# Column sums of a second softmax on VectorE's 32x32 transposes, and engine orders read from a table

## The chip, the cores and the metric

The kernel runs on one core of one Trainium2 chip. The metric is the device time of one execution in microseconds (us), median of several runs. The core's engines each work through a program of their own: TensorE (PE, with weight loads as PEld), VectorE (DVE), ScalarE (ACT), GpSimd (POOL) and SyncE (SP); they wait for each other by semaphores. POOL issues the loads from memory, SP issues the stores and the transposing copies.

## The reference

A two-stage attention is followed by a two-layer network with a quadratic knee as its activation. Shapes: 8 batches, 8 heads, 576 tokens of 64 channels, 32 landmark rows `p` per head; the network has widths 512, 2048, 512.

```python
def sm_attn(qq, kk, vv):
    s = scale * np.matmul(qq, kk.transpose(0, 1, 3, 2))
    s = s - np.max(s, axis=-1, keepdims=True)
    a = np.exp(s)
    a = a / (np.sum(a, axis=-1, keepdims=True) + 1e-09)
    return np.matmul(a, vv)
p_packed = sm_attn(p, k, v)
attn = sm_attn(q, p_packed, p_packed)
x = attn.transpose(0, 2, 1, 3).reshape(B * S, H * D)
h = x @ w_in
g = np.where(h >= 1, h, np.where(h <= -1, 0.0, (h + 1) ** 2 / 4))
out = g @ w_out
```

The second softmax is the one that the change touches: for each of 576 tokens and each of 8 heads it sums 32 numbers.

## The kernel before

**What is computed per batch.** The keys are brought into a transposed layout (`kT`), multiplied with the landmarks (tile `sp` or `s1`), and an exponential on ACT gives `ex` or `exn`. The packed values `pk` (32 rows per head) are copied to `ppT`, and their reciprocal sums are `rs`. From `ppT` two products are formed on PE: `mp`, the packed values already multiplied with `w_in`, which ACT or VectorE copies to `M`; and `s2` (shown as `s` in the profile), the second scores, 128 partitions by 576. The 128 partitions of `s2` are four heads times 32 landmarks, so the eight heads make two groups `g`. Partitions hold landmarks, the free axis holds the tokens. ACT takes `eT = exp(s2)` (line 723). The sum of a softmax runs here over 32 partitions of one head: PE multiplies `eT` with `onesblk`, a matrix of four 32x32 blocks of ones, which puts the sum on all 32 partitions (`sm`, line 728: two matmuls of 288 columns per group); ACT takes `ln` of it (line 732) and `rc = exp(-ln)` (line 737); VectorE forms `A = eT * rs * rc` (line 742).

**The hidden layer and the output.** For each of 16 slices `fi` of the hidden width PE forms `h` (line 814, four matmuls of 288 columns, reading `M` and `A`); ACT forms `x` from it (line 820); `t` is made from `x` by VectorE (line 828) or by ACT (line 830); VectorE writes `hT` (line 835). An output tile of 128 tokens is 16 matmuls `o` (line 889, 512 columns each, reading `hT` and `w_out_sb`), then a copy to `ob` (line 271, either engine) and a store on SP. There are 36 such tiles, 9 for each pair of batches; those of a pair run while the next batches are prepared. Buffers: three of two banks each in PSUM for `h`, `sm`, `s2`, `mp`, `pk` and others, two of one bank for `o`; four each of `x`, `t`, `eT` and `ob`.

**What sets the order.** Nothing is scheduled at run time. When the program is built, a planner (class `Plan`, lines 25 to 180) gives each step a rank, a length on each engine that may do it, its dependencies and its buffers, and picks the next step of each engine among those that are ready; ties within 0.05 us go by rank. The ranks come from the tables `AT`, `HID` and `OUT` (lines 228 to 244). The steps are emitted in the order of their planned starts, and each engine runs its own in that order. Before the first `o`, gaps of PE's plan are filled with matmuls on zeros (`warm`, line 939).

Of the kernel before, what the change touches and what calls it, by code (L numbers as in the profile page):

```python
# [11 lines left out]
class Task:  # L12
# [4 lines left out]
    def __init__(self, rank, ways, deps=(), takes=(), mode=None, behind=()):  # L17
        self.rank, self.ways, self.deps = rank, ways, list(deps)
        self.behind = [d for d in behind if d is not None]
        self.takes, self.frees, self.mode = list(takes), [], mode  # L20
        self.start = self.end = self.engine = None
        self.users = []


class Plan:
# [8 lines left out]
    CLAIM = 0.3  # L34
# [4 lines left out]
    def __init__(self, buffers):  # L39
# [8 lines left out]
    def add(self, rank, ways, deps=(), takes=(), mode=None, behind=()):  # L48
        t = Task(rank, ways, deps, takes, mode, behind)
        self.tasks.append(t)  # L50
        return t
# [38 lines left out]
    def run(self, slack):  # L90
        waiting = {id(t): len(t.deps) + len(t.behind) for t in self.tasks}
        started = defaultdict(list)
# [5 lines left out]
        ready = [t for t in self.tasks if not waiting[id(t)]]  # L98
        done = []

        def served(users):
            for u in users:
                waiting[id(u)] -= 1
                if waiting[id(u)] == 0:
                    ready.append(u)

        def finished(t):
# [5 lines left out]
            served(t.users)  # L113

        while len(done) < len(self.tasks):
            best = None
            found = defaultdict(list)
            left = {b: sorted(v) for b, v in self.slots.items()}
            for t in sorted(ready, key=lambda t: t.rank):
                at = max((d.end + self.LATENCY for d in t.deps), default=0.0)  # L120
                at = max([at] + [d.start + 0.001 for d in t.behind])
                need = defaultdict(int)
                for b in t.takes:
                    need[b] += 1
                short = any(len(left[b]) < n for b, n in need.items())
                wants = at < self.free["PE"] + self.CLAIM
                for b, n in need.items():
                    if not short:
                        at = max(at, left[b][n - 1] + self.LATENCY)
                    if wants:  # L130
                        del left[b][:n]
                if short:
                    continue
                for e in t.ways:
                    if e == "SP" and self.held is not None:
                        continue
                    start = max(self.free[e], at)
                    if e == "PE" and self.mode is not None and t.mode != self.mode:
                        start = max(start, self.free[e] + self.SWITCH)
                    found[e].append((start, t))  # L140
            for e, some in found.items():
                first = min(x[0] for x in some)
                at, t = min((x for x in some if x[0] <= first + slack.get(e, 0.0)), key=lambda x: (x[1].rank, x[0]))
# [7 lines left out]
            assert best is not None, "no step can take its buffers"  # L151
            at, t, e = best
            if e == "PE" and t.mode != self.mode:
                at = max(at, self.free[e] + self.SWITCH)
            ready.remove(t)
            keep, lasts = t.ways[e][:2]
            t.start, t.engine, t.end = at, e, at + lasts
# [6 lines left out]
            served(started[id(t)])  # L164
# [19 lines left out]
def kernel(  # L184
# [38 lines left out]
    SPLIT, AHALF, WPARTS, MPARTS, QLATE, ORDER3, ORDER = 2, 1, 1, 0, 1, 0, 2  # L223
# [3 lines left out]
    L1 = 15.967  # L227
    AT = [dict(kT=148.161, qT=275.48, sc=149.063, pk=-49.085, s2=-3.905, sm=-182.602, M=178.569, **{"M+": -129.863}),
          dict(kT=-39.644, qT=-48.123, sc=-66.351, pk=124.743, s2=170.079, sm=-187.478, M=-105.149, **{"M+": 146.812}),
          dict(kT=115.732, qT=51.477, sc=130.42, pk=237.931, s2=-181.084, sm=-29.758, M=169.369, **{"M+": -44.412}),  # L230
          dict(kT=29.446, qT=-25.092, sc=52.472, pk=243.839, s2=179.754, sm=-32.11, M=115.586, **{"M+": -71.343}),
          dict(kT=38.536, qT=86.402, sc=153.04, pk=258.796, s2=-13.152, sm=-43.327, M=-95.344, **{"M+": 110.184}),
          dict(kT=1.864, qT=113.754, sc=282.551, pk=400.409, s2=-26.009, sm=-92.874, M=125.845, **{"M+": 0.958}),
          dict(kT=126.633, qT=239.492, sc=-4.526, pk=382.024, s2=-90.437, sm=32.434, M=177.14, **{"M+": -62.453}),
          dict(kT=27.261, qT=148.76, sc=40.741, pk=216.362, s2=-45.985, sm=130.271, M=1.019, **{"M+": -201.613})]
    HID = [(27.4, 1.3921), (-10.054, 2.601), (22.49, 3.9747), (126.895, 4.8485), (231.121, 9.6612), (-18.141, 4.6461), (3.622, 15.8949), (451.41, 5.8147)]
    OUT = [[(235.954, -183.0), (268.544, -106.533), (35.947, 20.528), (122.624, -48.891)],
# [24 lines left out]
    plan = Plan(dict(BUFS, dma=8, exn=1))  # L262
# [52 lines left out]
    consts = plan.add(-1000, {"DVE": (2.4, 2.4, constants)})  # L315

    identity = plan.add(-998.5, {"POOL": (0.6, 1.25, lambda e: make_identity(nc, ident))})
# [3 lines left out]
    last_of = {"loads": identity}  # L321
# [8 lines left out]
    def dma(key, rank, emit, mb, takes=(), settle=0.9):  # L330
        t = plan.add(rank, {"DMA": (0.78, 2.1, emit, mb / 0.405, settle)}, takes=list(takes) + ["dma"])
        plan.release("dma", [t])
        chain("loads", t)
# [14 lines left out]
    def load(nm, b, rank):  # L348

        for i, hs in enumerate({("k", 0): [range(4, 8)], ("q", 0): Q0}.get((nm, b), [range(H)])):  # L350
# [3 lines left out]
            t = dma((nm, b, hs[0]), rank + 0.01 * i, emit, mb, [nm] if i == 0 else [], 0.9 if b < 2 else 1.1)  # L354
# [3 lines left out]
    def load_w_in(f, rank):  # L358

        parts = [(0, D), (D, P)] if WPARTS and f == 0 else [(0, P)]  # L360
        for i, (p0, p1) in enumerate(parts):
            dma(("w_in", f) + (i,) * (len(parts) - 1), rank + 0.01 * i,
# [4 lines left out]
    def load_w_out(f, rank):  # L367
# [610 lines left out]
```

## Time and profile before

| what | value |
|---|---|
| median of 3 runs | 244.42 us (243.48 to 244.64) |
| profiled execution, span from first to last instruction | 241.1 us |
| own time of the profiled execution | not on the page; the median of the runs lies 3.3 us above the span |
| instructions | 5370 |
| DVE busy, ACT busy in the 21.7 us behind 219.4 us | 3.69 us, 5.85 us |

A row of groups gives line, engine, operation, what is written and read, the count, then the busy time in us and the mean length of one in ns, then how long the engine sat idle just before them and what ended that. A row of the timeline or of the chain gives start and length in us. The length of one matmul contains its way through the array, so rows of several matmuls tell their rate: 33 matmuls `o` take 7.12 us, 0.2158 us each.

### The profile page before, as it was taken

The numbers are of one execution on the slowest core, as the hardware profiler recorded it, in microseconds if no ns is written. First come the engines' busy times: TensorE is split into PE (matmuls) and PEld (weight loads), VectorE is DVE, ScalarE is ACT, GpSimd is POOL, SyncE is SP. The second block draws the span as 40 slices with busy tenths as digits, with TensorE's granted clock in tenths as the row PEclk, the third lists the DMA queues.
The fourth block names the chain that finished last, engine by engine and source line by source line (L and its number), as shares of the span: only waits on it lengthen the run. The fifth ranks groups of instructions, "written<-read, shape, count | busy, mean of one in ns | idle before, by whom it ended". The sixth has DMA issues, their size and how long they took to land.

```text
span 241.1 us, 5370 instructions
## 1 busy us (share of the span) xinstructions
PE 233.3 (97%) x2117; PEld 133.9 (56%) x2154; DVE 177.6 (74%) x311; ACT 192.7 (80%) x342; POOL 31.4 (13%) x47
## 2 busy tenths in 40 slices
PE   8999999999999999999999999999999999999995
PEld 2646555466554665466645564465546644565454
DVE  4549997678967998789936898689999955899000
ACT  3779996988969985999776988999789988888111
POOL 8462006200220040030030003000000000000000
PEclk9999999999999999999999999999999999999999
DMA  7999999996999999999999999999930301202233
GB/s 158 196 206 207 206 205 205 197 241 132 125 198 149 234 164 251 152 221 221 194 165 246 233 141 147 161 141 226 191 94 4 85 5 44 71 21 65 65 87 90
DMA packets 64138, 37.03 MB, mean 154 GB/s; under 512 B 36720, under 2 KB 59632, under 8 KB 64112
## 3 DMA queue, kind: packets, MB, share of 16 engines
q0 software_dynamic: 24336, 18.25, 52.6%
q1 hardware_dynamic: 38960, 17.87, 36.7%
q10 hardware_dynamic: 816, 0.56, 0.8%
q8 instruction: 17, 0.28, 0.5%
q14 instruction: 9, 0.07, 0.1%
HBM read 37.22 MB, written 9.44 MB: 194 GB/s over the span
## 4 chain that ended last, share of the span: by engine, by line
PE 81%; DVE 6%; DMA 5%; ACT 4%; POOL 2%; issue 2%; POOLq 0%; ACTq 0%
PE o L889 48%; PE h L814 21%; DMA w_in_sb<-in_moe_w_in_dram 5%; DVE hT L835 4%; PE mp L686 3%; PE pk L619 2%; PE sm L728 1%; DVE t L828 1%; ACT x L820 1%; PE sp L528 1%; PE s L700 1%; ACT t L830 1%; POOL q L352 1%; ACT M L271 1%; PE o L942 1%
## 5 line engine op out<-in xcount | busy, mean ns | idle before, releaser
L889 PE MATMUL o<-w_out_sb,hT 128*128 128x512 bf16 (+2 forms) x574 | 140.9, 367 | 1.9 <-issue 0.6
L835 DVE SCALAR_TENSOR_TENSOR hT<-t 128x576 bf16<-128x576 f32 (+1 forms) x130 | 93.7, 746 | 4.3 <-ACT t L830 2.3
L820 ACT ACTIVATE x<-h 128x576 f32<-128x576 f32 (+1 forms) x130 | 78.6, 651 | 9.1 <-PE h L814 8.5
L889 PEld LDWEIGHTS <-hT 128*128 128x128 bf16 x608 | 55.8, 98 | 49.8 <-issue 6.1
L814 PE MATMUL h<-A,M 128*128 128x288 bf16 x512 | 78.5, 286 | 0.6 <-ACT M L271 0.3
L814 PEld LDWEIGHTS <-M 128*128 128x128 bf16 x512 | 49.9, 98 | 27.6 <-issue 1.1
L830 ACT ACTIVATE t<-x 128x576 f32<-128x576 f32 (+1 forms) x57 | 39.4, 693 | 0.6
L828 DVE TENSOR_SCALAR t<-x 128x576 f32<-128x576 f32 (+1 forms) x73 | 33.3, 456 | 7.1 <-ACT x L820 6.7
L271 ACT COPY ob<-o 128x512 f32<-128x512 f32 (+2 forms) x22 | 12.0, 552 | 17.0 <-PE o L889 16.9
L742 DVE SCALAR_TENSOR_TENSOR A<-eT,rs,rc 128x576 bf16<-128x576 bf16 (+1 forms) x18 | 12.8, 748 | 11.5 <-ACT rc L737 11.5
L271 ACT CAST M<-mp 128x1024 bf16<-128x1024 f32 (+1 forms) x20 | 19.1, 992 | 2.7 <-PE mp L686 2.7
L352 POOL DMA_DIRECT2D k<-in_k_dram x8 | 6.7, 843 | 87.8 <-DMA kT<-k 68.4
L271 DVE CAST M<-mp 128x1024 bf16<-128x1024 f32 (+1 forms) x13 | 15.3, 1180 | 3.1 <-PE mp L686 3.1
L271 DVE COPY ob<-o 128x512 f32<-128x512 f32 x16 | 10.8, 688 | 6.9 <-PE o L889 6.9
L723 ACT ACTIVATE eT<-s,rs 128x576 bf16<-128x576 f32 x16 | 11.1, 742 | 2.5 <-PE s L700 2.5
L942 PE MATMUL o<-zeros 128*128 128x512 bf16 (+1 forms) x35 | 10.5, 431 | 1.3 <-DVE zeros L307 1.2
L732 ACT ACTIVATE ln<-sm 128x576 f32<-128x576 f32 x16 | 10.3, 652 | 1.2 <-PE sm L728 0.7
L686 PE MATMUL mp<-w_in_sb,ppT 64*32 64x512 bf16 x256 | 10.9, 380 | 0.2
L271 ACT CAST ppT<-pk 64x128 bf16<-64x128 f32 x24 | 6.2, 260 | 5.7 <-PE pk L634 4.0
L737 ACT ACTIVATE rc<-ln 128x576 f32<-128x576 f32 (+1 forms) x18 | 10.4, 625 | 0.1
L352 POOL DMA_DIRECT2D v<-in_v_dram x8 | 6.2, 779 | 21.9 <-PE pk L624 15.2
L533 ACT ACTIVATE ex<-sp 96x768 bf16<-96x768 f32 (+1 forms) x12 | 8.1, 709 | 0.5 <-PE sp L528 0.4
(59 smaller groups left out, 116.7 us busy)
## 6 DMA issues: line engine op xcount, KB each, us to landing
v<-in_v_dram POOLq DMA_DIRECT2D x8, 576.0 KB, 11.6
out_dram<-ob SPq DMA_DIRECT2D x23, 192.0 KB, 4.5
k<-in_k_dram POOLq DMA_DIRECT2D x7, 576.0 KB, 8.7
q<-in_q_dram POOLq DMA_DIRECT2D x7, 576.0 KB, 12.8
out_dram<-ob SPq DMA_DIRECT2D x24, 128.0 KB, 2.9
w_out_sb<-in_moe_w_out_dram POOLq DMA_DIRECT2D x4, 512.0 KB, 19.7
w_in_sb<-in_moe_w_in_dram POOLq DMA_DIRECT2D x3, 512.0 KB, 15.2
out_dram<-ob SPq DMA_DIRECT2D x23, 64.0 KB, 4.5
```

The costliest lines, as they stand in the source:

```text
L271: i = (nc.vector.tensor_copy if e == "DVE" else nc.scalar.copy)(to, of)
L352: G_.dma_start(tokens(nm, b)[:, heads(hs)], rows_of(nm, b, hs))
L686: m = nc.tensor.matmul(have["mp", b, f][a * NP:(a + 1) * NP, g], have["ppT", b][r, g, a], w_in_sb[r, a, f * FW:(f + 1) * FW], start=True, ...
L723: nc.scalar.activation(have["eT", b, g], have["s2", b, g][:, :, :HALF], AF.Exp, scale=rs_of[b][:, g, 1:])
L742: V.scalar_tensor_tensor(have["A", b][:, g, xs], have["eT", b, g][:, xs], rs_of[b][:, g, :1], have["rc", b, g][:, xs], ALU.mult, ALU.mult)
L814: nc.tensor.matmul(have["h", b, fi][:, hf, :HALF], have["M", b][:, g, fi * P:(fi + 1) * P], have["A", b][:, g, hf], start=(g == 0), stop=( ...
L820: nc.scalar.activation(have["x", b, fi][:, hs[0]:hs[-1] + 1], have["h", b, fi][:, hs[0]:hs[-1] + 1, :HALF], AF.Prelu, bias=-1.0, alpha=0.5)
L828: V.tensor_scalar(t, x, 1.0, 0.0, ALU.add, ALU.max)
L830: nc.scalar.activation(t, x, AF.Relu, bias=1.0)
L835: V.scalar_tensor_tensor(dst, t, 1.0, t, ALU.min, ALU.mult)
L889: nc.tensor.matmul(have["o", key][:, :w], hT[:, fi, i * P:(i + 1) * P], w_out_sb[:, fi, cols], start=(fi == 0), stop=(fi == KF - 1))
L942: nc.tensor.matmul(o[:, :w], zeros[:, :P], zeros[:, :w], start=True, stop=True)
```

## The change

From batch 2 on the sum of a group is no longer made on PE. VectorE reduces `eT` over blocks of 32x32 with each block transposed (`reduced`: 576 columns become 18 sums per partition), takes their reciprocal in place, and a second instruction spreads the result back (`spread`: a transpose of 32x32 blocks from a broadcast read of the 18 numbers gives `rc`, 576 columns). `A` is formed as before. `sm`, `ln` and ACT's `rc` remain for batches 0 and 1 alone.

```diff
+    SUMS = 2
+    BLK = 32
...
+            def reduced(e, g=g):
+
+                have["r", b, g] = r = work.tile([P, X * HALF // BLK], f32, tag="r", name="r", bufs=4)
+                V.tensor_reduce(r, have["eT", b, g].rearrange("p x (k n) -> p (x k) n", n=BLK), axis=mybir.AxisListType.X,
+                                op=ALU.add, apply_transpose=True)
+                V.reciprocal(r, r)
+
+            def spread(e, g=g):
+                have["rc", b, g] = rc = new("rc", [P, X, HALF], f32)
+                V.transpose(rc.rearrange("p x (k n) -> p (x k) n", n=BLK),
+                            have["r", b, g].unsqueeze(2).to_broadcast([P, X * HALF // BLK, BLK]))
...
-            t_s = last_sums = plan.add(r + 0.01, {"PE": (0.245, 0.41, sums)}, [t_e, consts], ["w", "ln", "rc"])
-            t_l = plan.add(r + 0.02, {"ACT": (0.59, 0.645, ln)}, [t_s])
...
+            if b < SUMS:
+                t_s = last_sums = plan.add(mine, {"PE": (0.245, 0.41, sums)}, [t_e, consts], ["w", "ln", "rc"])
+                t_l = plan.add(mine, {"ACT": (0.59, 0.645, ln)}, [t_s])
...
+            else:
+                n = 0
+                t_s = plan.add(mine, {"DVE": (0.93, 0.99, reduced)}, [t_e])
+                t_r = plan.add(mine, {"DVE": (0.66, 0.72, spread)}, [t_s], ["rc"])
```

The second part replaces the ranks. A table `ORDER` gives every step its place in its engine's line, and a letter (`A` or `D`) where ACT and VectorE could both do it; `Plan.run` no longer chooses, it takes the head of each line:

```diff
-            for t in sorted(ready, key=lambda t: t.rank):
...
+        lines = defaultdict(list)
+        for t in sorted(self.tasks, key=lambda t: t.rank):
+            lines[t.engine].append(t)
...
+    ORDER = """
+    first 0 0 0 1 3D 1A
+    load 0 2 1 3 4 5 6 7 10 8 9 11 13 12 15 14 16 20 19 18 17 21 23 22 27 25 26 24 28 29 32 31 33 30 35 34
```

So the order of all engines is another one, also where the sums are not concerned. The instructions by count (whole tiles; `t`, `M` and `ob` also move between the two engines):

| instructions | before | after |
|---|---|---|
| PE `sm`, 288 columns | 32 | 8 |
| PE on zeros, 512 columns / 256 columns | 34 / 4 | 34 / 8 |
| ACT `ln` / ACT `rc`, 576 columns | 16 / 14 | 4 / 2 |
| VectorE `r` reduce, `r` reciprocal, `rc` transpose | 0, 0, 0 | 12, 12, 12 |
| `t` of 576 columns on VectorE / ACT | 70 / 56 | 88 / 38 |
| `M` of 1024 columns on VectorE / ACT | 12 / 19 | 6 / 25 |
| `ob` of 512 columns on VectorE / ACT | 16 / 19 | 10 / 25 |
| PE `o` between batch 2's, 3's, 5's last `s2` and its first `h` | 17, 17, 17 | 25, 24, 23 |
| the same for batches 4, 6, 7 | 31, 19, 33 | 32, 26, 25 |
| PE `o` behind the last `h`, 512 / 256 / 128 columns | 70 / 16 / 32 | 88 / 16 / 32 |

VectorE in batch 2, from `rs` to the copies `vv` of the next batch, before (the numbers tell the tiles of one batch apart):

```order
L669 RECIPROCAL rs_1215<-pk_1216 128x4
L271 CAST M_1284<-mp_1285 128x2x512
L271 COPY ob_1307<-o_1000 128x512
L742 SCALAR_TENSOR_TENSOR A_1353<-eT_1295,rs_1215,rc_1321 128x576
L742 SCALAR_TENSOR_TENSOR A_1353<-eT_1301,rs_1215,rc_1351 128x576
L271 CAST M_1284<-mp_1342 128x2x512
L602 COPY vv_1384<-v_1212 96x4x6x64 x2
```

The same place of VectorE in the changed kernel:

```order
L722 RECIPROCAL rs_1186<-pk_1187 128x4
L326 COPY ob_1251<-o_1084 128x512
L326 CAST M_1274<-mp_1275 128x2x512
L786 TENSOR_REDUCE r_1295<-eT_1285 128x18
L788 RECIPROCAL r_1295<-r_1295 128x18
L786 TENSOR_REDUCE r_1303<-eT_1291 128x18
L788 RECIPROCAL r_1303<-r_1303 128x18
L792 STREAM_TRANSPOSE rc_1313<-r_1303 128x576
L792 STREAM_TRANSPOSE rc_1344<-r_1295 128x576
L807 SCALAR_TENSOR_TENSOR A_1349<-eT_1291,rs_1186,rc_1313 128x576
L807 SCALAR_TENSOR_TENSOR A_1349<-eT_1285,rs_1186,rc_1344 128x576
L655 COPY vv_1363<-v_1133 96x4x6x64 x2
```

Six instructions have come in between the copies and the two `A`, and one of the two copies of `M` has gone to ACT.

ACT at the same place, before, from the exponentials to the first `x` of batch 2:

```order
L723 ACTIVATE eT_1295<-s2_1266,rs_1215 128x576
L723 ACTIVATE eT_1301<-s2_1275,rs_1215 128x576
L732 ACTIVATE ln_1310<-sm_1303 128x576
L732 ACTIVATE ln_1317<-sm_1312 128x576
L737 ACTIVATE rc_1321<-ln_1310 128x576
L737 ACTIVATE rc_1351<-ln_1317 128x576
L271 CAST M_1284<-mp_1324 128x2x512
L271 CAST M_1284<-mp_1333 128x2x512
L820 ACTIVATE x_1376<-h_1370 128x576
```

And in the changed kernel:

```order
L776 ACTIVATE eT_1285<-s2_1265,rs_1186 128x576
L776 ACTIVATE eT_1291<-s2_1256,rs_1186 128x576
L326 COPY ob_1310<-o_1137 128x512
L326 COPY ob_1342<-o_1069 128x512
L326 CAST M_1274<-mp_1333 128x2x512
L326 CAST M_1274<-mp_1324 128x2x512
L326 CAST M_1274<-mp_1315 128x2x512
L892 ACTIVATE x_1378<-h_1366 128x576
```

The four passes `ln` and `rc` are gone, and two copies of outputs and one of `M` stand in their place.

POOL's first loads, before: `k` of batch 0, all of its `v`, then its `q` in three parts, and later `w_out_sb` ahead of the next `k`.

```order
L352 DMA k_107<-in_k_dram 96x4x384
L352 DMA v_109<-in_v_dram 96x8x384
L352 DMA q_112<-in_q_dram 96x4x384
L352 DMA q_112<-in_q_dram 96x2x384 x2
L363 DMA w_in_sb_73<-in_moe_w_in_dram 64x4x512 x2
```

In the changed kernel:

```order
L406 DMA k_107<-in_k_dram 96x4x384
L406 DMA q_109<-in_q_dram 96x4x384
L406 DMA v_112<-in_v_dram 96x8x384
L406 DMA q_109<-in_q_dram 96x2x384 x2
L417 DMA w_in_sb_73<-in_moe_w_in_dram 64x4x512 x2
```

The first part of `q` has gone ahead of `v`. On SP the transposing copies `kT` and `qT` of batch 2 now stand ahead of all stores; before, eight stores stood ahead of them.

More of the change, by code (lines that the diff above doesn't have):

```diff
@@ L17, in __init__, with in_rows @@
     def __init__(self, rank, ways, deps=(), takes=(), mode=None, behind=()):
[L18 removed]
+        self.rank, self.ways, self.deps = float(rank.rstrip("AD")), ways, list(deps)
         self.behind = [d for d in behind if d is not None]
         self.takes, self.frees, self.mode = list(takes), [], mode
[L21 removed]
+        self.start = self.end = None
+        self.engine = next(e for e in ways if len(ways) == 1 or e[0] == rank[-1])
         self.users = []
+def in_rows(text):
+    rows = {}
+    for word in text.split():
+        if word[0].isalpha():
+            row = rows.setdefault(word, [])
+        else:
+            row.append(word)
+    return rows
 class Plan:
@@ L97, in run @@
                 started[id(d)].append(t)
-        ready = [t for t in self.tasks if not waiting[id(t)]]
+        lines = defaultdict(list)
+        for t in sorted(self.tasks, key=lambda t: t.rank):
+            lines[t.engine].append(t)
+        lines = {e: lines[e][::-1] for e in ("PE", "ACT", "DVE", "POOL", "SP", "DMA")}
         done = []
[L101 to L105, printed above, removed]
         def finished(t):
@@ L150, in run @@
                 continue
-            assert best is not None, "no step can take its buffers"
+            assert best is not None, "the order of an engine waits for itself"
             at, t, e = best
-            if e == "PE" and t.mode != self.mode:
-                at = max(at, self.free[e] + self.SWITCH)
-            ready.remove(t)
+            lines[e].pop()
             keep, lasts = t.ways[e][:2]
-            t.start, t.engine, t.end = at, e, at + lasts
+            t.start, t.end = at, at + lasts
             self.free[e] = at + keep
@@ L921 @@
         first = 0 if b % 2 == 0 else 4
-        for j, (start, span) in enumerate(OUT[b]):
-            widths = (256, 128, 128) if (b, first + j) == (B - 1, 8) else (d_model,)
-            output(b // 2, first + j, start, span / KF / len(widths), widths)
-    order = plan.run({"PE": 0.05, "ACT": 0.05, "DVE": 0.05, "SP": 0.0, "DMA": 0.0})
+        for i in range(first, first + 4 + b % 2):
+            output(b // 2, i, (256, 128, 128) if (b, i) == (B - 1, 8) else (d_model,))
+    order = plan.run()
     first_o = min(t.start for t in o_of.values())
```

290 lines of the change are left out of this document (172 added, 118 removed), and 7 rows, old and new, of the table OUT.

## The prediction

> **What bounds the kernel now.** I read the shares of the engines first, then what PE waited for, then the chain that ended last.
>
> ```profile
> PE 233.3 (97%) x2117; PEld 133.9 (56%) x2154; DVE 177.6 (74%) x311; ACT 192.7 (80%) x342; POOL 31.4 (13%) x47
> ```
>
> PE is busy in 97% of the span, but busy can mean spread out, so the list of PE's waits is the one that decides:
>
> ```profile
> PE o L942 <- DVE zeros L307: 1.2, 1, 1.2
> PE o L889 <- issue: 0.6, 4, 0.2
> PE sp L528 <- DVE kT L271: 0.4, 1, 0.4
> PE h L814 <- ACT M L271: 0.3, 1, 0.3
> PE sp L528 <- ACT ex L533: 0.2, 1, 0.2
> ```
>
> That is all of it: 2.7 us, of which 1.2 are the very start. And PE runs at its rate: in the chain, listed in order of time, a run of matmuls shows its length per matmul.
>
> ```profile
> 201.37 0.49 PE sm L728 x4
> 219.47 7.12 PE o L889 x33
> 226.65 11.48 PE o L889 x84
> 238.15 0.27 ACT ob L271
> ```
>
> 33 matmuls `o` in 7.12 us are 0.2158 us each, four `sm` in 0.49 us are 0.1225 us each. So from about 20 us until 238.1 us the time is the sum of PE's matmuls at these rates, with hardly a hole. The chain says the same by shares:
>
> ```profile
> PE 81%; DVE 6%; DMA 5%; ACT 4%; POOL 2%; issue 2%; POOLq 0%; ACTq 0%
> ```
>
> Anything taken off PE's list shortens the span one for one, as long as the other engines still deliver. Anything put on VectorE or ACT costs nothing until one of its results is late at PE.
>
> **What goes: the sums on PE.** Twelve groups (six batches, two groups) lose two matmuls of 288 columns each: 24 x 0.1225 = **2.94 us**. They stand in PE's line among matmuls `o` that run back to back, so nothing hides them.
>
> **What comes on PE.** The changed program has four more matmuls of 256 columns on zeros ahead of the first `o` (42 in place of 38). Half of 0.2158 each, they are **0.43 us** of filling. I count it in full, since fillings stand where PE had nothing to do and more of them mean a longer start. The bounds are 0 (they fill a hole that was there) and 0.43.
>
> **What goes on ACT.**
>
> ```profile
> L732 ACT ACTIVATE ln<-sm 128x576 f32<-128x576 f32 x16 | 10.3, 652 | 1.2 <-PE sm L728 0.7
> L737 ACT ACTIVATE rc<-ln 128x576 f32<-128x576 f32 (+1 forms) x18 | 10.4, 625 | 0.1
> L830 ACT ACTIVATE t<-x 128x576 f32<-128x576 f32 (+1 forms) x57 | 39.4, 693 | 0.6
> L828 DVE TENSOR_SCALAR t<-x 128x576 f32<-128x576 f32 (+1 forms) x73 | 33.3, 456 | 7.1 <-ACT x L820 6.7
> L271 ACT CAST M<-mp 128x1024 bf16<-128x1024 f32 (+1 forms) x20 | 19.1, 992 | 2.7 <-PE mp L686 2.7
> L271 DVE CAST M<-mp 128x1024 bf16<-128x1024 f32 (+1 forms) x13 | 15.3, 1180 | 3.1 <-PE mp L686 3.1
> L271 ACT COPY ob<-o 128x512 f32<-128x512 f32 (+2 forms) x22 | 12.0, 552 | 17.0 <-PE o L889 16.9
> L271 DVE COPY ob<-o 128x512 f32<-128x512 f32 x16 | 10.8, 688 | 6.9 <-PE o L889 6.9
> ```
>
> ACT loses 12 x (0.652 + 0.625) = 15.3 us and 18 of the `t`, 18 x 0.693 = 12.5 us; it takes 6 copies `M`, 6.0 us, and 6 `ob`, 3.3 us. Some 18 us less, so ACT falls from 192.7 to about 174 us. By itself that is worth nothing, since PE waited 0.5 us for ACT in all.
>
> **What comes on VectorE.** A transposing reduce and a spreading transpose do not occur in this trace. The rows nearest to a pass over 576 columns:
>
> ```profile
> L742 DVE SCALAR_TENSOR_TENSOR A<-eT,rs,rc 128x576 bf16<-128x576 bf16 (+1 forms) x18 | 12.8, 748 | 11.5 <-ACT rc L737 11.5
> 70.96 0.18 DVE L669 RECIPROCAL rs<-pk 128x4 f32<-128x4 f32 x1
> ```
>
> The bounds for either pass are 0.456 us (`t`, the fastest row of 576 columns) and 1.18 us (`M`, a pass over 1024 columns). I take 0.75 us, the row of `A`, because it has the same columns and reads the same `eT`; the reciprocal of 18 columns I take at 0.18 us, as on 4 columns. A group then adds 0.75 + 0.18 + 0.75 = 1.68 us, twelve of them 20.2 us. With 18 `t` more (8.2 us), 6 `M` fewer (7.1 us) and 6 `ob` fewer (4.1 us), VectorE goes from 177.6 to about **195 us**. [...]
>
> Is there room for 195 us? Behind the last `h` VectorE did little:
>
> ```profile
> 219.40:241.10 21.70, 18.66 (x118) 10.11 (x117) 3.69 (x7) 5.85 (x12) 0.00 (x0) 1.00 0.31 85
> 156.20:180.00 23.80, 23.52 (x213) 13.20 (x215) 22.38 (x36) 21.66 (x40) 0.00 (x0) 1.00 0.97 159
> ```
>
> (columns: length, then PE, weight loads, VectorE, ACT, POOL). So VectorE now does 174 us in the first 219 us, 79%. In the changed kernel 88 `o` of 512 columns stand behind the last `h` in place of 70, 3.9 us more, so the last `h` comes near 238.6 - 3 - 22.4 = 213 us; VectorE has to do about 192 us by then, 90%. That is tight, not full. The second row above shows a stretch where VectorE was at 22.38 of 23.80 us, 94%, and PE still had 23.52: such a filling has been carried without PE losing anything.
>
> **The wait that matters: the first `h` of a batch.** Each engine has a fixed line, so a late `A` stops everything behind the first `h` of its batch: the other `h`, the `o` mixed with them, and with them ACT's `x`. Batch 2 in the timeline:
>
> ```profile
> 71.33 0.44 PE L700 MATMUL s<-qT,ppT 64*32 64x288 bf16 x16
> 71.72 1.37 ACT L723 ACTIVATE eT<-s,rs 128x576 bf16<-128x576 f32 x2 [0.83 <-PE s L700]
> 73.23 1.33 ACT L732 ACTIVATE ln<-sm 128x576 f32<-128x576 f32 x2
> 74.46 1.25 ACT L737 ACTIVATE rc<-ln 128x576 f32<-128x576 f32 x2
> 75.17 1.55 DVE L742 SCALAR_TENSOR_TENSOR A<-eT,rs,rc 128x576 bf16<-128x576 bf16 x2 [1.29 <-ACT rc L737]
> 76.96 0.65 PE L814 MATMUL h<-A,M 128*128 128x288 bf16 x4
> ```
>
> `A` ends at 75.17 + 1.55 = 76.72, and `h` starts 0.24 us later: just in time. VectorE had idled 1.29 us ahead of `A`, in all batches 11.5 us (the row of `A` above); that idle time goes, because VectorE now does the work it waited for. From the start of `s2` to `h` were 5.63 us. In the changed order 25 `o` stand there in place of 17, and four `sm` are gone: 5.63 + 8 x 0.2158 - 0.49 = 6.87 us. The new chain: the first `eT` ends at 71.72 + 0.74 = 72.46, 1.13 us behind the start of `s2`; then on VectorE, one after the other, two reduces and reciprocals, two transposes and two `A`: 2 x 0.93 + 2 x 0.75 + 1.55 = 4.91 us; then 0.24 us. That is 6.28 us against 6.87: **0.6 us to spare**. With 24 and 23 `o` in batches 3 and 5 it is 0.4 and 0.2 us. PE covers the longer chain with `o` that must be done anyway. If this cover is missed by a given time, each of six batches pays it.
>
> VectorE writes no `hT` during that block. It did not before either: `M`, `ob`, two `A`, `M` and `vv` stood together there, and now it is some 2 us longer, while one `M` has left.
>
> **What else moves.** `v` of batch 0 is loaded behind the first part of `q`:
>
> ```profile
> L624 PEld LDWEIGHTS <-v 96*64 96x64 bf16 x96 | 1.7, 113 | 0.9 <-DMA v<-in_v_dram 0.5 <-issue 0.4
> 2.28 0.79 POOL L352 DMA_DIRECT2D v<-in_v_dram  x1
> POOL k L352 <- DMA kT<-k: 68.4, 4, 19.4
> ```
>
> The first `pk` waited 0.5 us for `v`, and one issue takes POOL 0.79 us, so the start can lose up to 0.8 us; in PE's line other work now stands ahead of `pk`. I take 0, with 0 to 0.8 as the bounds. The `w_out_sb` loads move back by one or two places; the first `o` moves back too, behind 20 more `h` matmuls. On SP two transposing copies pass eight stores; POOL waited 68.4 us for such a copy (the last row above) and PE, by its list, never, so this is put at nothing. Three small copies at the very end change from ACT (0.27 us in the chain) to VectorE; put at nothing.
>
> **The sum.** 241.1 - 2.94 + 0.43 = 238.6 us of span. The page gives no own time of the profiled execution; the median of the runs is 3.3 us above its span (244.42 - 241.1), and this part is not touched: **241.9 us**, 1.0% less.
>
> **The rivals.**
>
> - *The new orders also close holes at the start* (chance 0.12). The filling of 7.8 us (34 x 0.2158 + 4 x 0.108) is time in which PE had no work; the order is another one there too. Against it: there is not less filling but more. If 1.5 us went, the time would be 240.4 us, from 240.0 to 241.0.
> - *The spread is slow* (0.20). It reads each of 18 numbers 32 times over, which no row shows. At the upper bound of 1.18 us the two transposes lengthen the chain by 0.86 us, over the 0.2 to 0.6 us to spare by 0.3 to 0.7 us; at 0.4 us for each of six batches 2.4 us come back: 244.3 us, about no change; with less of it 243.2, with more 245.6. For it: `A` stood just in time. Against it: VectorE's rows of 576 columns lie at 0.456 and 0.748 us, none above. [...] That the sums were hidden all along would also give no change; against that, the chain itself runs through `sm`.
> - *The whole block comes late at the first `h`* (0.18, slower). If reduce and transpose both cost 1.18 us, the chain is 1.72 us longer and each of six first `h` waits 1.1 to 1.5 us: some 7.5 us, 238.6 + 7.5 + 3.3 = 249.4 us. It decides from where six waits eat the 2.5 us gained, 0.42 us each: with 0.2 to 0.6 us to spare, that is a pass of 0.9 to 1.0 us in place of 0.75. At a filling of 90% VectorE can also reach the block late by its own queue, with the same effect. Against it: the 94% stretch above, and no row of a 576-column pass above 0.75 us.
>
> That the change does not do what it says is not at issue: the counts of instructions show the sums gone from PE.
>
> **How the numbers follow.** Forecast 0.50, for 241.0 to 243.2 us; the rivals as given. Half a percent, 1.2 us, is about what a measurement of this kernel can tell from no change. Faster: 0.50 + 0.12 = 0.62. Within: 0.20. Slower: 0.18. A range that leaves out the slower rival reaches from 240.0 to 245.6 us and takes in the bounds of the filling, of `v` and of a slow spread.
>
> **What would show it.** If right: PE's `sm` falls to 8 matmuls, PE's list of waits stays within about 3 us, the span is near 238.6 us, VectorE's busy time is near 195 us and ACT's near 174 us, the reduce and the transpose take about 0.75 us, and the first `h` of batches 2 to 7 starts within 0.3 us of its `A`, without a hole on PE. A hole on PE that `A` ends in each of these batches would show the third rival, and with a transpose near 1.1 us alone the second. An end that is right with more waiting on PE and a shorter start would mean right for the wrong reason.

## The result, and the profile after

The changed kernel takes **246.9 us** (median of 4 runs, 245.31 to 247.31), the kernel before 244.19 us (4 runs beside it, 243.48 to 244.64). The ratio is 1.0117 with a 95% interval of 1.0072 to 1.0162: slower by about 1.2%, where 1.0% faster was forecast. Six more runs gave 245.92 us, ratio 1.0095 [1.0057, 1.0133] (e12 below). (Ratios leave out runs over 1.5% above the fastest of the same kernel, medians are of all runs.)

The profiled execution took 245.31 us, its span is 243.5 us. It is the fastest of the four: what the median has on top of it stands in no trace. The shares of the engines, changed kernel:

```profile
PE 233.6 (96%) x2134; PEld 132.0 (54%) x2134; DVE 191.7 (79%) x358; ACT 176.3 (72%) x307; POOL 31.1 (13%) x47
```

VectorE and ACT stand where they were forecast (195 and 174 us). PE lost 2.94 - 0.43 = 2.5 us of work and yet its busy time is no shorter, in a span 2.4 us longer. (The two busy times can't be compared to tenths: the trace before has 574 matmuls `o` for 608 weight loads, the one after 608.) What PE waited for, in the changed kernel (us in total, times, longest):

```profile
PE o L965 <- ACT ob L326: 1.5, 2, 1.2
PE o L1016 <- DVE zeros L362: 1.2, 1, 1.2
PE mp L739 <- DVE rs L722: 1.1, 1, 1.1
PE o L965 <- DVE hT L907: 0.7, 1, 0.7
PE sp L582 <- DMA kT<-k: 0.7, 1, 0.7
PE h L886 <- DVE M L326: 0.6, 2, 0.4
PE tp L525 <- DMA q<-in_q_dram: 0.6, 1, 0.6
PE h L886 <- ACT x L892: 0.4, 1, 0.4
```

That is all: 6.8 us in place of 2.7. No row is a wait for `A`. The new passes on VectorE, from the groups by line (in front of the bar the shapes and the count, behind it busy us and mean ns):

```profile
L786 DVE TRANSPOSE_TENSOR_REDUCE r<-eT 128x18 f32<-128x576 bf16 x12 | 9.0, 747 | 0.3 <-ACT eT L776 0.3
L792 DVE STREAM_TRANSPOSE rc<-r 128x576 f32<-128x576 f32 x12 | 8.5, 743 | 0.1
L788 DVE RECIPROCAL r<-r 128x18 f32<-128x18 f32 x12 | 3.2, 266 | 0.4
```

0.75 us each for reduce and transpose, as forecast. Where the time is lost shows in the busy time by stretches (length, then PE, weight loads, VectorE, ACT, POOL, granted clock, DMA share, GB/s), before:

```profile
0.00:57.00 57.00, 54.05 (x576) 30.65 (x587) 40.26 (x84) 45.24 (x83) 19.35 (x32) 1.00 1.18 196
57.00:160.00 103.00, 101.74 (x946) 59.08 (x962) 82.91 (x140) 89.45 (x156) 12.05 (x15) 1.00 1.19 186
```

and in the changed kernel:

```profile
0.00:57.00 57.00, 54.34 (x602) 31.35 (x603) 44.24 (x94) 44.61 (x80) 19.15 (x32) 1.00 1.27 188
57.00:160.00 103.00, 98.70 (x922) 55.58 (x921) 84.92 (x151) 81.93 (x141) 11.95 (x15) 1.00 1.15 190
160.00:200.00 40.00, 40.00 (x368) 22.32 (x367) 37.22 (x70) 32.46 (x59) 0.00 (x0) 1.00 0.37 90
```

The start is as it was, and in the 40 us from 160 us on PE never stands. Between 57 and 160 us it stands 4.30 us in place of 1.26. Up to 160 us the DMA share is over 1 in both kernels (1.18 and 1.19 before, 1.27 and 1.15 after: the recorded times of the packets overlap); behind it the share falls to 0.37 in the changed one. The chain says what the holes hang on. Changed kernel, in order of time (start, us, what):

```profile
83.61 9.41 DMA v<-in_v_dram
...
102.81 9.41 DMA v<-in_v_dram
...
119.88 6.52 DMA out_dram<-ob
```

Two kinds of stop can be read off it. First, the copy `vv` waits for a load of `v` of 9.4 us. Second, a store takes 6.5 us to leave its buffer, and ACT's copy `ob` waits for that. The timeline of the changed kernel has who waits behind them (in brackets the idle time ahead):

```profile
93.11 0.56 DVE L655 COPY vv<-v 96x1536 bf16<-96x1536 bf16 x1 [2.28 <-DMA v<-in_v_dram]
93.58 0.17 DVE L722 RECIPROCAL rs<-pk 128x4 f32<-128x4 f32 x1
93.81 0.41 PE L739 MATMUL mp<-w_in_sb,ppT 64*32 64x512 bf16 x8 [1.05 <-DVE rs L722]
112.31 0.56 DVE L655 COPY vv<-v 96x1536 bf16<-96x1536 bf16 x1 [2.67 <-DMA v<-in_v_dram]
126.49 0.58 ACT L326 COPY ob<-o 128x512 f32<-128x512 f32 x1 [2.68 <-DMA out_dram<-ob]
127.13 0.38 PE L965 MATMUL o<-w_out_sb,hT 128*128 128x512 bf16 x1 [1.24 <-ACT ob L326]
```

The copy `vv` stands in VectorE's line **ahead of** `rs`, VectorE idles 2.28 us in front of it, and PE's `mp` waits for `rs`, though neither needs this `v`. Before, the two stood the other way round:

```profile
96.47 0.18 DVE L669 RECIPROCAL rs<-pk 128x4 f32<-128x4 f32 x1
97.61 0.56 DVE L602 COPY vv<-v 96x1536 bf16<-96x1536 bf16 x1 [0.95 <-DMA v<-in_v_dram]
```

VectorE waited for this load then too, but with `rs` done. The load itself has not become late: it is issued at 83.61 us and landed by 93.02 us, where before it was issued at 85.46 us and `vv` could start at 97.61 us. It is the copy that has moved ahead. The hole of 0.7 us on `hT` (at 124.64 us) comes behind the second such wait, the 2.67 us at 112 us: VectorE is busy 9.90 of the 10 us from 115 to 125 us, with the new passes among its `hT`. The row is gone both in e1, without the passes, and in e4, with `vv` later.

ACT waits 2.68 us for an older store to free one of the four `ob`, and PE's next `o` waits for that copy. Where the stores are, the timeline tells, in the changed kernel:

```profile
101.06 2.00 SPq L983 DMA_DIRECT2D out_dram<-ob  x4
102.81 0.69 DVE L326 COPY ob<-o 128x512 f32<-128x512 f32 x1
109.51 6.38 SPq L554 DMA_TRANSPOSE kT<-k  x1
116.00 2.95 SPq L554 DMA_TRANSPOSE qT<-q  x1
119.05 8.84 SPq L983 DMA_DIRECT2D out_dram<-ob  x6
```

and before:

```profile
102.79 0.61 ACT L271 COPY ob<-o 128x512 f32<-128x512 f32 x1
104.33 3.44 SPq L908 DMA_DIRECT2D out_dram<-ob  x6
113.69 6.14 SPq L500 DMA_TRANSPOSE kT<-k  x1
119.93 3.08 SPq L500 DMA_TRANSPOSE qT<-q  x1
```

Before, the tile copied to `ob` at 102.79 us could leave with the six stores that went out ahead of the two transposing copies. In the changed kernel only four go out there, and the tile copied at 102.81 us (output 13) is stored behind the copies: 6.38 + 2.95 us of SP's queue pass first, and its buffer is held from 102.81 to 126.4 us. That this store is the one that ACT waits for is read from the order of the queue; e5 tests it.

### The profile page after: what moved, and what is told of

The parts are those of the page before. It is cut to its first block, busy times and chain, and to the rows that moved or that the text cites. A ratio compares the mean times of both kernels' runs of the same rounds, so it can differ in the third digit from the quotient of the medians.

```text
span 243.5 us, 5413 instructions
## 1 busy us (share of the span) xinstructions
PE 233.6 (96%) x2134; PEld 132.0 (54%) x2134; DVE 191.7 (79%) x358; ACT 176.3 (72%) x307; POOL 31.1 (13%) x47
## 4 chain that ended last, share of the span: by engine, by line
PE 62%; DMA 22%; DVE 10%; issue 2%; ACT 1%; POOL 1%; SPq 0%; POOLq 0%; DVEq 0%; ACTq 0%
PE o L965 34%; PE h L886 19%; DMA v<-in_v_dram 11%; DMA kT<-k 6%; DVE hT L907 4%; DMA out_dram<-ob 3%; DMA qT<-q 2%; PE mp L739 2%; PE o L1016 2%; DVE A L807 1%; PE pk L672 1%; DVE M L326 1%; PE tp L525 1%; DVE t L900 1%; PE pk L677 1%
## 5 line engine op out<-in xcount | busy, mean ns | idle before, releaser
L965 PE MATMUL o<-w_out_sb,hT 128*128 128x512 bf16 (+2 forms) x608 | 144.3, 368 | 2.2 <-ACT ob L326 1.5
L900 DVE TENSOR_SCALAR t<-x 128x576 f32<-128x576 f32 (+1 forms) x90 | 40.2, 463 | 12.6 <-ACT x L892 12.1
L326 ACT COPY ob<-o 128x512 f32<-128x512 f32 x25 | 14.5, 588 | 26.4 <-PE o L965 21.7
L902 ACT ACTIVATE t<-x 128x576 f32<-128x576 f32 (+1 forms) x40 | 26.6, 672 | 0.2
L326 ACT CAST M<-mp 128x1024 bf16<-128x1024 f32 (+1 forms) x26 | 25.1, 1006 | 1.7 <-PE mp L739 1.7
L326 DVE COPY ob<-o 128x512 f32<-128x512 f32 (+2 forms) x13 | 7.9, 609 | 15.4 <-PE o L965 15.3
L655 DVE COPY vv<-v 96x1536 bf16<-96x1536 bf16 x12 | 6.3, 551 | 5.2 <-DMA v<-in_v_dram 5.2
L326 DVE CAST M<-mp 128x1024 bf16<-128x1024 f32 (+1 forms) x7 | 8.0, 1146 | 2.9 <-PE mp L739 2.9
L786 DVE TRANSPOSE_TENSOR_REDUCE r<-eT 128x18 f32<-128x576 bf16 x12 | 9.0, 747 | 0.3 <-ACT eT L776 0.3
L792 DVE STREAM_TRANSPOSE rc<-r 128x576 f32<-128x576 f32 x12 | 8.5, 743 | 0.1
```

The source lines that it names most:

```text
L326: i = (nc.vector.tensor_copy if e == "DVE" else nc.scalar.copy)(to, of)
L900: V.tensor_scalar(t, x, 1.0, 0.0, ALU.add, ALU.max)
L902: nc.scalar.activation(t, x, AF.Relu, bias=1.0)
L965: nc.tensor.matmul(have["o", key][:, :w], hT[:, fi, i * P:(i + 1) * P], w_out_sb[:, fi, cols], start=(fi == 0), stop=(fi == KF - 1))
```

## The experiments

Theory: the sums' gain is there, and the new order of copies and stores gives it back through waits for loads and stores. Rivals: the passes on VectorE are what makes PE late; or PE isn't the bound and the sums were never worth 2.9 us. In "before" I give the median of the kernel before on the same chip.

### Is it the work on VectorE? (e1, e7)

```diff
+        V.memset(rc_one.rearrange("p x n -> p (x n)"), 1.0 / NP)
...
-                V.tensor_reduce(r, have["eT", b, g].rearrange("p x (k n) -> p (x k) n", n=BLK), axis=mybir.AxisListType.X,
-                                op=ALU.add, apply_transpose=True)
-                V.reciprocal(r, r)
...
-                have["rc", b, g] = rc = new("rc", [P, X, HALF], f32)
-                V.transpose(rc.rearrange("p x (k n) -> p (x k) n", n=BLK),
-                            have["r", b, g].unsqueeze(2).to_broadcast([P, X * HALF // BLK, BLK]))
+                have["rc", b, g] = rc_one
```

> Leaves out the twelve reduces, reciprocals and transposes on VectorE (A uses a constant in place of the sums), everything else in the same order. Theory B (VectorE's new block makes the first h late, or fills VectorE): PE's holes vanish and the time falls from about 246.9 by 4 to 5 us, to about 242. Theory A (VectorE and ACT stand behind a v load that lands late and a store that ends late): only the hole of about 1.1 us at 153 to 157 us can go, so 245 to 246 us.

Here `A` multiplies by a constant in place of the reciprocal sums. Measured: 248.7 us (247.23 to 250.4), before 243.68, ratio 1.0199 [1.0133, 1.0266]. Neither forecast came: without the 12 reduces, reciprocals and transposes the kernel is not faster, and by the medians 1.8 us slower still. Its PE waited most for this:

```profile
PE o L962 <- ACT ob L326: 3.7, 2, 3.1
```

VectorE fell to 172.8 us and the hole at the stores grew. Behind that hole of 3.1 us the granted clock of PE fell (the number ahead of the last two):

```profile
130.00:133.00 3.00, 3.00 (x13) 1.66 (x12) 0.69 (x1) 1.88 (x4) 0.00 (x0) 0.50 1.29 230
```

Half the clock for 3 us is an estimated 1.5 us of PE's work, so a part of the 248.7 us is this and no wait. Taking the passes out doesn't bring the time back; that they cost nothing this run alone can't show. Why the hole grows when VectorE has less to do, the runs don't settle.

> As e5, without the twelve reduces, reciprocals and transposes on VectorE (A uses a constant). If the block is covered by the outputs that PE has meanwhile: within 0.7 us of e5. If the block costs time at the first h: 1.5 us or more below e5.

The same without the passes on the version e5 (below): 243.33 us (241.63 to 247.73), before 243.39, ratio 0.9989 [0.9965, 1.0013]; e5 itself has 244.52 and 0.9953. By the medians that is 1.2 us less, by the ratios 0.4% more, and both spread over 6 us and more: no gain from leaving out the passes that can be told, and no choice between the forecasts of 0.7 and of 1.5 us. Stronger than both is e4 below, which keeps all the passes and is faster than the kernel before.

### Is it the late loads and stores? (e2, e3, e4, e5, e11)

e2 moves the first half of `vv` of batches 4 and 5 behind the two `A` of the batch ahead, by its ranks:

```diff
-    a4 12 14 280 134 281 135 130 142 296 150A 152A 158 323 158 171 173 175 157 169 170 176 159A 338 161A 162A 163A
+    a4 12 14 280 134 281 135 141.5 142 296 150A 152A 158 323 158 171 173 175 157 169 170 176 159A 338 161A 162A 163A
...
-    a5 17 18 371 172 173 22 155 177 399 201D 194D 202 433 195 209 211 213 196 210 212 214 197A 449 215D 200A 199A
+    a5 17 18 371 172 173 22 176.5 177 399 201D 194D 202 433 195 209 211 213 196 210 212 214 197A 449 215D 200A 199A
```

> The first half of the copy vv of batches 4 and 5 moves behind the two A of the batch before, nothing else. Theory A: the holes on PE behind VectorE's waits for v (1.3 us at 92.6 us, about 0.7 us at 117 us) go, 1 to 3 us less, 244 to 246 us. Theory B: no change, 246 to 247 us.

Measured: 248.53 us (248.37 to 249.11), before 243.68, ratio 1.0194 [1.0148, 1.0241]. The wait for `rs` went (VectorE's waits for `v` fell from 5.2 to 0.5 us), and the time rose, where 244 to 246 us were expected. PE's first wait is now a store's, in one hole:

```profile
PE o L965 <- ACT ob L326: 5.6, 2, 5.2
```

and the stretches around it are

```profile
120.00:125.00 5.00, 3.62 (x17) 1.57 (x16) 4.44 (x8) 2.32 (x3) 1.56 (x3) 1.00 0.98 172
125.00:128.00 3.00, 0.00 (x0) 0.00 (x0) 0.00 (x0) 0.00 (x0) 0.74 (x1) 1.00 1.18 239
128.00:131.00 3.00, 2.20 (x9) 1.27 (x9) 0.00 (x0) 1.20 (x2) 0.00 (x0) 0.56 1.27 192
131.00:134.00 3.00, 3.00 (x20) 1.84 (x19) 0.69 (x1) 2.38 (x5) 0.00 (x0) 0.87 1.22 229
```

All engines but POOL stand from 125 to 128 us, with a DMA share of 1.18, and behind the hole the granted clock is 0.56 and 0.87. I read it so, and e4 bears it out: PE gets to the second stop earlier once the first is gone, and waits there longer. It is not the whole: the store ends later too, so that ACT's copy starts at 128.17 us in place of 126.49, for which no run gives the reason. Taking away one wait is no test of a theory that names two.

e3 leaves the order and gives ACT and VectorE six buffers `ob` for four, so that a late store stops nobody:

```diff
-    BUFS = dict(w=3, o=2, k=1, q=2, v=1, vv=1, kT=2, qT=2, ex=2, ks=2, ppT=2, M=2, A=2, eT=4, ln=2, rc=2, x=4, t=4, ob=4)
+    BUFS = dict(w=3, o=2, k=1, q=2, v=1, vv=1, kT=2, qT=2, ex=2, ks=2, ppT=2, M=2, A=2, eT=4, ln=2, rc=2, x=4, t=4, ob=6)
```

> Six buffers for ob in place of four, the same order. Theory A: ACT's wait for a store (2.7 us at 124 to 126 us) and PE's holes behind it (0.8 and 1.4 us) go, 1.5 to 2.5 us less, about 244.5 to 245.5 us. Theory B: no change.

Measured: 245.3 us (243.28 to 247.48), before 243.68, ratio 1.0051 [1.0016, 1.0086]. In the profile the waits for stores are gone, `mp <- rs` (0.8) and `o <- hT` (0.7) stay. By the ratio that is about half of the loss against the kernel before, by the medians of all runs less (1.6 of 2.7 us stay). The profiled run is the fastest of the ten, 243.28 us, so it doesn't show what the others wait for.

e4 is both edits:

> Both the later vv copies and six ob buffers. Theory A: 3 to 4.5 us less than the change, 242.5 to 244 us, at or below the kernel before. Theory B: no change, 246 to 247 us.

Measured: **242.07 us** (241.72 to 245.96), before 243.68, ratio 0.9932 [0.9904, 0.9961]; span 240.1 us. The longest of PE's waits:

```profile
PE o L1016 <- DVE zeros L362: 1.2, 1, 1.2
PE h L886 <- DVE M L326: 0.9, 2, 0.6
PE sp L582 <- DMA kT<-k: 0.8, 1, 0.8
...
```

All rows together are 3.9 us in place of 6.8, with neither `rs` nor `ob` among them, and PE is busy 101.54 of the 103 us from 57 to 160. It beats both kernels. That it comes within 0.2 us of the forecast 241.9 is in part luck, since the kernel before was faster on this chip too: 1.6 us less than before were measured here, 2.5 were forecast.

e5 keeps four buffers and issues one store (of output 13) earlier on SP, ahead of the transposing copies, with e2's edit:

```diff
-    o13 241 243 245 250 253 257 259 263 264 267 268 270 271 272 278 279 144D 19
+    o13 241 243 245 250 253 257 259 263 264 267 268 270 271 272 278 279 144D 16.5
```

> As e2 (later vv copies, four ob buffers), and one store of an output tile (o13) is issued on SP ahead of the two transposing copies kT and qT of batch 5 in place of behind them. Theory A (the place of stores among the transposing copies on SP keeps the ob buffers): PE's hole of 3 to 5 us near 125 us goes, as with six buffers, 241.5 to 243.5 us, against 248.5 for e2. Theory B (VectorE's block): no difference to e2. Theory C (the stores are slow because the DMA engines are full, whatever the order): 245 us or more.

Measured: 244.52 us (240.91 to 248.76), before 243.39; the ratio is 0.9953 [0.9924, 0.9982], but it rests on the six lowest of twelve runs. The place of that one store moves the profiled span from 246.6 (e2) to 241.0 us, and PE's wait for ACT's `ob` falls from 5.6 to 1.0 us, so it was this store; a wait of 1.6 us for VectorE's `ob` comes in its place, and from run to run the time differs by up to 248.76 - 240.91 = 7.9 us. The median is 4.0 us below e2, and lies between the forecasts of theory A and theory C.

> All three repairs: later vv copies, six ob buffers, the early store. If the repairs act on the same holes: as e4, 241.5 to 242.5 us, and no run above 244. If stores still bound something: 0.5 us or more below e4.

e4 with that store early too: 242.62 us (240.38 to 246.47), before 243.65, ratio 0.9946 [0.9918, 0.9974]. Beside e4 nothing can be told; one run of twelve lies above the 244 us that were named as the limit.

### Fewer loads, on both kernels (e10, e13)

The sharpest test leaves the order and the buffers alone, and only lightens the DMA engines: the loads of `v` of batches 3 to 7, 576 KB each, are left out, and `vv` reads batch 2's.

```diff
+                if nm == "v" and b >= 3:
+                    have[nm, b] = have[nm, 2]
+                    return
```

> The changed kernel, same order, without the loads of v of batches 3 to 7 (their copies vv read the v of batch 2): five transfers of 576 KB as stored fewer for the DMA engines. If the holes come from transfers that end late: the waits for v go and the stores near 120 us end sooner, PE's holes there fall below 1 us, 240.5 to 242.5 us. If the place of the store behind the transposing copies on SP alone decides: the hole of 1.4 to 5 us at 125 us stays, 244 us or more.

Measured: **241.56 us** (241.22 to 242.34), before 243.65, ratio 0.9919 [0.9894, 0.9944]. The DMA share from 57 to 160 us is 1.00 in place of 1.15. Of PE's waits for `rs` and `ob` this is left (the profile of e10):

```profile
PE o L968 <- ACT ob L326: 0.6, 1, 0.6
```

> The kernel before, same order, without the loads of v of batches 3 to 7 (their copies vv read the v of batch 2). If transfers cost the kernel before nothing, because PE is full: no change, 243.2 to 244.2 us. If they cost it as much as the changed kernel: 4 us less, about 240 us.

The same edit in the kernel before: 243.9 us (242.77 to 244.28), before 243.32, ratio 1.0012 [0.999, 1.0033]. The kernel before has nothing to gain from fewer loads; the changed one gains 4.4 us (245.92 to 241.56, on the same chip), and its ratio agrees with the 0.99 that was forecast. So its loss hangs on transfers, and the kernel before loses nothing to them. How, e10 can't say: without the loads `vv` has nothing to wait for, wherever it stands, and ACT still waits 2.5 us for stores, of which 0.6 us reach PE.

### Is PE the bound, and are the sums worth 2.9 us? (e6, e14, e8)

e6 puts 24 matmuls of 288 columns on zeros back into e4's line of `o`:

```diff
+                        if pr >= 1 and i < 4:
+                            for _ in range(2):
+                                nc.tensor.matmul(have["o", key][:, :HALF], onesblk, zeros[:, :HALF], start=True, stop=True)
```

> As e4 (later vv copies, six ob buffers) with 24 more matmuls of 288 columns on zeros on PE, two ahead of each of twelve output tiles: as many as the sums that were taken off PE; nothing else. If PE is the bound once the two waits are gone: 24 x 0.1225 = 2.9 us more than e4, 244.5 to 245.5 us. If the sums were hidden: as e4, about 242 us.

Measured: 244.55 us (244.35 to 244.7), before 243.39, ratio 1.0049 [1.003, 1.0069]. Against e4's 0.9932 that is 1.0049 / 0.9932 = 1.0118, of 243.4 us some 2.9.

e14 takes the sums out of the kernel before from batch 2 on and puts nothing in their place; `ln` reads `eT`, so that ACT does what it did.

```diff
+                if b >= 2:
+                    return
...
-                nc.scalar.activation(have["ln", b, g], have["sm", b, g][:, :, :HALF], AF.Ln)
+                of = have["eT", b, g] if b >= 2 else have["sm", b, g][:, :, :HALF]
+                nc.scalar.activation(have["ln", b, g], of, AF.Ln, scale=float(NP) if b >= 2 else 1.0)
```

> The kernel before, same order, without the 24 matmuls of the sums from batch 2 on (ln reads 32 times eT in place of them), nothing added on VectorE. If the old order has transfers to spare: 24 x 0.1225 = 2.9 us less, about 240.7 us. If any kernel whose PE is 2.9 us faster waits for transfers: 242.5 us or more, with waits of PE behind kT, v or ob.

Measured: 240.77 us (240.41 to 241.05), before 243.32, ratio 0.9881 [0.9848, 0.9914]: 2.9 us less by the ratio, 2.6 by the medians, where 24 x 0.1225 = 2.94 was worked out. Both ways the term has its size, and in the old order it comes out whole.

> The kernel before with six ob buffers and the order unchanged on every engine. Theory A says that the kernel before has no wait on stores at PE, so no change, 243.2 to 244.2 us. If buffers of ob held it back too, 1 us or more less.

e8 gives the kernel before six `ob` and leaves its order: 243.98 us (242.8 to 245.72), before 243.39, ratio 1.0028 [1.0004, 1.0051]. In the old order more buffers give nothing, so that e4 is faster than the kernel before is not due to them alone.

### Was another order needed at all? (e15, e9)

e15 puts the passes into the kernel before with nothing moved: reduce and reciprocal where `sums` stood, the transpose where ACT's `rc` stood.

```diff
+                if b >= SUMS:
+                    have["r", b, g] = r = work.tile([P, X * HALF // BLK], f32, tag="r", name="r", bufs=4)
+                    V.tensor_reduce(r, have["eT", b, g].rearrange("p x (k n) -> p (x k) n", n=BLK), axis=mybir.AxisListType.X,
+                                    op=ALU.add, apply_transpose=True)
+                    V.reciprocal(r, r)
+                    return
```

> The sums of the change in the order of the kernel before: the reduces take the place in which the sums stood, the transposes that of ACT's rc, no step is moved, ACT's freed time is left empty. The first h of a batch keeps its 17 outputs as cover (5.1 us without the sums), the new chain takes about 6.3 to 7 us with the copies that stand between. If the cover decides: PE waits 1.2 to 1.9 us for A at six first h, 8 to 11 us, against 2.9 us taken off: 248 to 252 us. If VectorE's chain overlaps enough: 241 to 243 us.

Measured: 248.43 us (247.93 to 249.09), before 243.49, ratio 1.0194 [1.0146, 1.0242]. Its first wait of PE is the one that the prediction feared:

```profile
PE h L828 <- DVE A L756: 5.4, 9, 1.2
```

Nine waits of an `h` for its `A`, the longest 1.2 us: 5.4 us in all, less than the 8 to 11 expected. With 17 `o` in front of it the longer chain isn't covered (1.1 to 1.2 us of wait in batches 2, 3 and 5); batches 4 and 7, with 31 and 33 there, wait 0 and 0.2 us, and with the change's 25 in batch 2 there is no wait either. So the moved `o` are needed.

e9 leaves the choice of order to the planner of the kernel before, with the passes as steps of its own (ranks r + 0.01 for the reduce, + 0.02 for the transpose, + 0.04 for `A`).

> The sums of the change alone, put into the kernel before: its ranks and its scheduler stay, so the order is the scheduler's own and another one again wherever the new steps shift it. If the loss lies in the order of the table alone and the sums are worth their 2.9 us: 240.5 to 242 us. If any order fails once PE runs ahead of loads and stores: 243.5 us or more, with waits of PE behind v or ob.

Measured: 247.26 us (245.17 to 250.68), before 243.65, ratio 1.0137 [1.0101, 1.0173]. The profiled one, the fastest of the six with a span of 243.4 us, waits most in two places:

```profile
PE h L835 <- DVE A L755: 2.1, 2, 1.8
PE sp L530 <- DMA kT<-k: 2.0, 1, 2.0
```

One wait is the late `A`, the other again a transfer.

### Once more (e12)

> The changed kernel once more, as the reference for the others on one chip: 245 to 247.5 us. If a run has a hole of over 3 us on PE near 125 us, the granted clock falls for some us behind it and the run is the longer for both; a run with 2 us of holes there keeps the clock at 1.0.

The changed kernel unaltered, beside e9 to e11: 245.92 us (244.17 to 247.17), before 243.65, ratio 1.0095 [1.0057, 1.0133]. The loss came again. The profiled run (246.25 us) keeps its clock at 1.00 and waits longest for `rs` (1.4 us in all), `ob` (0.9) and `hT` (0.7) again. It has no long hole, so this run doesn't test what was expected of one: the clock behind a hole stands at 0.50 (3.1 us, e1), 0.56 (5.2 us, e2) and 1.00 (1.24 us, the changed kernel).

## Why the prediction was wrong

**What bounds the kernel.** Right: PE. 24 matmuls more cost e4 2.9 us, 24 fewer save the kernel before 2.9 (e6, e14).

**What goes and comes on PE.** Right in size: -2.94 us is what e14 shows. Up to 57 us PE was busy 54.34 us in place of 54.05, with 4 more fillings in it: what is left for other work differs by 0.1 us, and no run singles out the 0.43.

**ACT and VectorE.** Right: 176.3 and 191.7 us busy against 174 and 195. The reduce has 747 ns and the transpose 743 ns against 750. Only the reciprocal of 18 columns was mis-sized, 266 ns for 180; the difference is 1 us of VectorE over twelve.

**The wait that matters.** Right that it is covered, and tight. Batch 2 of the changed kernel, timeline:

```profile
67.83 0.44 PE L753 MATMUL s<-qT,ppT 64*32 64x288 bf16 x16
73.09 1.50 DVE L807 SCALAR_TENSOR_TENSOR A<-eT,rs,rc 128x576 bf16<-128x576 bf16 x2
74.70 1.14 PE L886 MATMUL h<-A,M 128*128 128x288 bf16 x8
```

From `s2` to `h` are 74.70 - 67.83 = 6.87 us, the cover worked out. `A` ends at 74.59, 6.76 us behind `s2`, where 6.28 - 0.24 = 6.04 were worked out: the chain is 0.7 us longer and the spare all but used up, but `h` comes 0.11 us behind and PE has no wait for `A`. VectorE comes late to the block: its first reduce starts at 69.69 us, behind a copy `M`, and not at about 69.1, when `eT` is there. e15 shows that this cover was needed.

**What else moves.** Here it failed: "On SP two transposing copies pass eight stores; POOL waited 68.4 us for such a copy (the last row above) and PE, by its list, never, so this is put at nothing." I priced the copies that moved ahead and not the stores that fall behind such copies: a store holds one of four `ob`, ACT or VectorE waits for the buffer (ACT 2.68 us), and PE for ACT (1.24 us). The store that cost PE 1.2 us is a later one than those named there, output 13 behind the copies of batch 5. The `vv` that the table of ranks had put ahead of `rs` I had not listed at all; in the piece of VectorE's line shown with the change `vv` stands at the end, and I did not follow the line into batches 3 and 4. In place of nothing the two stops cost PE 1.1 us on `rs`, 1.5 on `ob` and 0.7 on `hT`. That PE had not waited for a transfer before was read as room, and it was room only in that order. The DMA share alone would not have told: from 57 to 160 us it is 1.19 in the kernel before and 1.19 in e4, which is faster, against 1.15 in the changed kernel.

**The sum.** 238.6 us of span were forecast and 243.5 came, 4.9 more. Of these, 4.1 stand in PE's list of waits (6.8 against 2.7). But the 0.6 of `issue` in the list before are no waits: they stand where that trace lacks records of matmuls, and the trace after, which lacks none, has no such row. Without them the lists differ by 4.7, which leaves 0.2. The 3.3 us from span to time were mis-sized: in the changed kernel's profiled run they are 245.31 - 243.5 = 1.8, which is also the median of all executions on record, with at most 2.9; the rest is the distance of the profiled execution from the median of the runs. That waits for transfers account for the loss is shown by e10 with its control e13, and by e4. What stays open is the split between loads and stores: the two stops shift into each other (e2).

**The rivals.** None was the one that came. The sign named for the second one, a transpose near 1.1 us, rests on no row of 576 columns and no run shows such a pass; the spread took 743 ns. The slower one had the right sign and another cause: it wanted holes that `A` ends, and there are none, so the sign is no merit of it. A DMA rival, the changed order with the two stops, was missing.

**What would show it.** `sm` at 8, VectorE and ACT and the passes came as written. The first `h` did in batches 2, 3 and 6; it starts 0.4 us behind its `A` in batch 7 and 1.2 to 1.3 us in batches 4 and 5, held there by `ob` and by `M`. "PE's list of waits stays within about 3 us" was the line that failed, and it led straight to the rows with `rs` and `ob`.

## What to carry to other kernels

When a change brings its own order, list for each engine everything that now stands behind something it did not stand behind before, and ask of each what it waits for: an instruction that wants a load stops all behind it on its engine, also those that need no load (here `rs` behind `vv`: VectorE stood 2.28 us and PE 1.05 us). A store belongs to the input side of the engine that fills its buffer; a store that falls behind other issues on its queue comes back as a wait for a buffer (here 2.68 us of ACT and 1.24 us of PE). And where a busy engine hides transfers, neither a list of waits without a DMA nor the DMA share (1.19 before, 1.15 after) says how much room there is; leaving some loads out of both kernels (e10, e13) measured it in two runs: 4.4 us for the changed kernel, nothing for the kernel before.

## What the runs showed of the hardware

- In e1 and e2 the granted clock fell behind a long hole of PE. In e2 PE stood 5.2 us for one `o`, up to 128.8 us, and the clock was 0.56 from 128 to 131 us and 0.87 from 131 to 134 us; in e1 it stood 3.1 us, and the clock was 0.50 from 130 to 133 us. Behind the changed kernel's hole of 1.24 us (126 us) it stayed at 1.00. The two long holes so cost more than themselves, in e1 by the estimated 1.5 us.
- A transpose that reads each of 18 numbers 32 times over takes 743 ns for 576 columns of f32, no more than the reduce that reads 576 of bf16 (747 ns).
- The stores took unequal times to land: the one on the chain 6.52 us, at a DMA share of 1.08 from 119.88 to 126.40 us; the page has a median of 2.4 us for 23 issues of 192 KB in the changed kernel, and of 4.5 us in the kernel before, where PE waited for none.
